# Loads reordered at the start of an attention-plus-experts kernel, and a last tile split 384 + 128

## The chip, the cores and the metric

The kernel runs on one core of a Trainium2 chip. The core has a matrix engine (TensorE, "PE" in the profile, with "PEld" for its weight loads), a vector engine (VectorE, "DVE"), an engine for activation functions (ScalarE, "ACT"), a general one (GpSimd, "POOL") and one that only issues transfers (SyncE, "SP"). Transfers between the device memory (DRAM) and the on-chip memory run on 16 DMA engines. TensorE writes its results into PSUM, from where VectorE or ScalarE copy them out. Each engine goes through its own instructions in order and waits where data or a buffer is missing. The metric is the time of one execution on the device in microseconds, as the median of several runs.

## What is computed

Attention over 4 batches, 8 heads, 768 positions and 64 channels per head, followed by a mixture of four experts over all 3072 tokens:

```python
scores = (q @ k.T) / sqrt(64)             # per batch and head
# heads 0, 2, 6: causal; heads 1, 3, 4, 5, 7: the first 4 keys and the last 64 alone
a = softmax(where(mask, scores, -1e9))
x = (a @ v), heads side by side           # 3072 x 512
p = domain_probs / domain_probs.sum(-1)   # 3072 x 4
for e in range(4):
    h = relu(x @ w1[e])                   # 512 -> 1024
    out += p[:, e] * (h @ w2[e])          # 1024 -> 512
```

All inputs are 32-bit floats; the weights, queries, keys and values are turned into 16-bit floats on their way into the chip.

## The kernel before

The tokens are worked on in eight groups of 384 (half a batch each). A *unit* is one group with one expert: a first layer of 32 matmuls of 384 columns (line L895), 16-bit results of which ScalarE writes as `hs` after the ReLU, and a second layer of 24 matmuls of 512 columns (L919), whose result VectorE scales and adds into `acc`. Group 0's attention comes first, alone; each later group's attention is dealt out between the matmuls of the group before it.

GpSimd issues the loads that change the type. The order in which they stand in the program is their order in one queue. `landed` makes GpSimd wait until a tile is there, so that not too many loads stand in the queue at once:

```python
load_v(0, 0, [2, 1, 3, 4, 6])
load_w1(0, 0, F)                # expert 0, first layer: two loads of 512 KB
load_v(0, 0, [5, 7])            # values of heads 5 and 7, group 0
load_w2(0)                      # expert 0, second layer: 1024 KB
# [...] memory set to zero and to ones
load_w1(1, 0, F)
landed(w1_of(0))
load_triples(k, k16, 0, 1)      # group 1's keys, 384 KB
load_triples(q, qt16, 0, 1)     # group 1's queries, 384 KB
landed(w2_of(0))
load_w2(1)
landed(qt16[0:1, 0, 0, 0:1])
load_v(0, 1, RH)                # group 1's values, heads 0, 2, 6
load_w1(2, 0, F)
landed(w2_of(1))
load_v(0, 1, SH[:2])
load_w2(2)
# [...]
```

Group 0's attention ends with the values of heads 5 and 7. `warm_up` puts matmuls on a tile of zeros ahead of some of them, which keep TensorE occupied while it would wait for data; their results are not used:

```python
def values(h):
    # [...]
    if first:
        warm_up(ps, {3: 4, 4: 4, 5: 6, 7: 10}.get(h, 0), 256)
    # [...] matmuls of v_tile and es (L726), then Ln, Exp and a scaling: xT

yield from values(5)
x_transposes(6)                 # head 6's result turned round (L703)
yield from values(7)
```

Group 1's attention begins by turning its queries and keys round on TensorE (L516), two heads at a time. The results of the first two pairs go to the pool `pV`, which has two buffers; VectorE copies them out (queries L525; keys L532 and L548):

```python
def transposes(hp):
    for x, is_k in ((qt16, 0), (k16, 1)):
        ps = bank() if hp > 1 else pV.tile([P, 512], FP32, name="pV", bufs=2)
        # [...] six matmuls against the identity (L516)
        if not is_k:
            nc.vector.tensor_copy(out=qTs[...], in_=...)   # L525
            yield t_ns
            continue
        # [...] two copies per pair, to kR (L532) or kS (L548)
        yield 2 * t_ns
```

`bank()` is the pool `pA` with four buffers, which scores and first layers share. Where group 1's attention begins and ends among group 0's units is set in the main loop; a `UNIT` is the nominal time of one unit, and each step of the attention is let in when the matmuls so far have passed its share:

```python
begin = {0: 1.15, 1: 1.0}.get(g, 0.0) * UNIT
end = {0: 3.5}.get(g, 0.90 * n_units) * UNIT
```

Group 2's keys are turned round by the DMA engines (`kR<-kRr`), as are those of all later groups.

The last tile of the last unit is made in two parts, so that the first part is scaled and stored while TensorE makes the second:

```python
def last_tile(e, nt, hs, acc):
    for n, eng in enumerate((nc.sync, nc.scalar)):
        cols = slice(n * DM // 2, (n + 1) * DM // 2)
        # [...] eight matmuls of 256 columns (L863)
        # [...] VectorE: acc += p * ps (L870)
        eng.dma_start(out=out[nt * P : (nt + 1) * P, cols], in_=acc[:, cols])
```

Of the kernel before, what the change touches and what calls it, by code (L numbers as in the profile page):

```python
# [17 lines left out]
def kernel(  # L18
# [33 lines left out]
    nc = tc.nc  # L52
    P = 128
    B, H, S, D = q.shape
    E, DM, F = moe_w1.shape
# [101 lines left out]
    def own_v(h):  # L157
        return half(PLACE[h][1])
# [10 lines left out]
    def v_tiles(b, c, h):  # L169

        if RETR[h]:
            return vR[b % 2][:, 3 * c : 3 * c + 3, RH.index(h), :]
        if b:
            return windows(vSf, c)[:, :, SH.index(h), :]
        return vS[:, c, :, SH.index(h), :]
# [10 lines left out]
    def rows_of(x, b, h, c):  # L186
        return x[b, h, c * CH : (c + 1) * CH, :].rearrange("(j p) d -> p j d", p=P)

    def tiles_of(x, b, h, c):
        return x[b, h, c * CH : (c + 1) * CH, :].rearrange("(t r) d -> r t d", r=TK)  # L190

    def windows_of(x, b, h, c):

        assert b > 0
        first = ((b * H + h) * S + c * CH - WO) * D
        return bass.AP(x.tensor, x.offset + first, [[D, P], [WQ * D, WT], [1, D]])
# [13 lines left out]
    def load_triples(x, dst, b, c):  # L210

        gp.dma_start(
            out=dst.rearrange("p h j d -> p h (j d)"),
            in_=x[b, :, c * CH : (c + 1) * CH, :].rearrange(
                "h (p j) d -> p h (j d)", j=3
            ),
        )
# [47 lines left out]
    def load_v(b, c, heads):  # L265
        for h in heads:
            t = v_tiles(b, c, h)
            if RETR[h]:
                gp.dma_start(out=t[:, :, 0:D], in_=rows_of(v, b, h, c))  # L269
            elif b:  # L270
                gp.dma_start(  # L271
                    out=t[:, :, own_v(h)], in_=windows_of(v, b, h, c)
                )
            else:
                gp.dma_start(  # L275
                    out=t[R0:P, :, own_v(h)],
                    in_=tiles_of(v, b, h, c),
                )
# [18 lines left out]
    def load_w1(e, f0, f1):  # L297
        x = moe_w1[e].rearrange("(u c d) f -> u d c f", u=2, c=DMP)
        for u in range(2):
            gp.dma_start(  # L300
                out=w1sb[half(u), e * DMP : (e + 1) * DMP, f0:f1],
                in_=x[u, :, :, f0:f1],
            )

    def load_w2(e):
        gp.dma_start(
            out=w2sb[:, e * FTP : (e + 1) * FTP, :],
            in_=moe_w2[e].rearrange("(fo fi) d -> fi fo d", fi=P),
        )
# [41 lines left out]
    for h in range(H):  # L351
        if h == 2:
            nc.sync.dma_start(
                out=v_s32, in_=v[0, :, 0:NS, :].rearrange("h r d -> r h d")
# [13 lines left out]
        eng = nc.scalar if h < HP else nc.sync  # L368
        eng.dma_start(out=q32[:, :, h, :], in_=rows_of(q, 0, h, 0))
    nc.sync.dma_start(  # L370
        out=probs, in_=moe_domain_probs.rearrange("(t p) e -> p t e", p=P)
# [14 lines left out]
    def warm_up(ps, n, cols):  # L386
        for _ in range(n):
            nc.tensor.matmul(
                out=ps[:, 0:cols], lhsT=warm[:, 0:P], rhs=warm[:, 0:cols],
                start=True, stop=True,  # L390
            )
# [53 lines left out]

    mask_c(bC, 0.0, -60000.0)
    mask_s(bS[:, 0:2, :], 2, 0.0, -60000.0)
    load_v(0, 0, [2, 1, 3, 4, 6])
    load_w1(0, 0, F)
    load_v(0, 0, [5, 7])  # L450
    load_w2(0)
    zero(gp, kR[0][:, 1, :, :, :])
    zero(gp, kS[:, 1, :, :, :].rearrange("p t s x -> p s t x"))
# [2 lines left out]
    qt16 = att.tile([P, H, 3, D], FP16, name="q16", bufs=2)  # L456

    def landed(x):

        gp.tensor_copy(out=seen, in_=x)  # L460

    def w1_of(e):
        return w1sb[D : D + 1, e * DMP, 0:1]

    def w2_of(e):
        return w2sb[0:1, e * FTP, 0:1]

    load_w1(1, 0, F)
    landed(w1_of(0))
    load_triples(k, k16, 0, 1)  # L470
    load_triples(q, qt16, 0, 1)
    landed(w2_of(0))
    load_w2(1)
    landed(qt16[0:1, 0, 0, 0:1])
    load_v(0, 1, RH)
    load_w1(2, 0, F)
    landed(w2_of(1))
    load_v(0, 1, SH[:2])
    load_w2(2)
# [15 lines left out]
    def attention(b, c):  # L495
        g = b * NCH + c
# [212 lines left out]
        def values(h):  # L709
            if RETR[h]:  # L710
                yield from values_r(h)
                return
            ct, u = PLACE[h]
            if first and u == 1:
                ps = pO.tile([P, 512], FP32, name="pO", bufs=2)
            else:
                ps = pV.tile([P, 512], FP32, name="pV", bufs=2)
            if first:
                warm_up(ps, {3: 4, 4: 4, 5: 6, 7: 10}.get(h, 0), 256)
            work = []  # L720
            for es, parts in es_of[h]:
                for t, o, q0, nq in parts:
                    work.append((es, t, o, q0, nq))
            ns = 0
            for n, (es, t, o, q0, nq) in enumerate(work):
                nc.tensor.matmul(  # L726
                    out=ps[:, q0 : q0 + nq],
                    lhsT=v_tile(b, c, h, t),
                    rhs=es[:, o : o + nq],
                    start=(n == 0),  # L730
                    stop=(n == len(work) - 1),
                    skip_group_check=True,
                )
                ns += mm_ns(nq)
                if ns > 300 and n < len(work) - 1:
                    yield ns
                    ns = 0

            r, o = half(u), half(1 - u)
            pair = first and h in (3, 4)  # L740
            if not pair or u == 0:
                rc_of[0] = att.tile([P, CH], FP32, name="rc", bufs=4)
            rc = rc_of[0]
            nc.scalar.activation(  # L744
                out=rc[r, :], in_=ps[o, 0:CH], func=AF.Ln, bias=eps[o, :]
            )

            def scale(r=r, ps=ps):
                nc.vector.tensor_tensor(  # L749
                    out=xT[g][r, ct, :], in0=ps[r, 0:CH], in1=rc[r, :], op=ALU.mult  # L750
                )

            if not pair:
                nc.scalar.activation(out=rc[r, :], in_=rc[r, :], func=AF.Exp, scale=-1.0)  # L754
                later(scale)
            elif u == 0:
                scale_of[0] = scale
            else:
                nc.scalar.activation(out=rc, in_=rc, func=AF.Exp, scale=-1.0)
                later(scale_of[0])  # L760
                later(scale)

            yield ns + (600.0 if g == 1 else 0.0)
# [92 lines left out]

    def last_tile(e, nt, hs, acc):

        for n, eng in enumerate((nc.sync, nc.scalar)):
            cols = slice(n * DM // 2, (n + 1) * DM // 2)  # L860
            ps = pV.tile([P, 512], FP32, name="pV", bufs=2)
            for ft in range(FTP):
                nc.tensor.matmul(  # L863
                    out=ps[:, 0 : DM // 2],
                    lhsT=hs[:, ft, 2 * P : 3 * P],
                    rhs=w2sb[:, e * FTP + ft, cols],
                    start=(ft == 0),
                    stop=(ft == FTP - 1),
                )
            nc.vector.scalar_tensor_tensor(  # L870
                out=acc[:, cols], in0=ps[:, 0 : DM // 2],
                scalar=p_sb[:, nt, e : e + 1], in1=acc[:, cols],
                op0=ALU.mult, op1=ALU.add,
            )
            eng.dma_start(out=out[nt * P : (nt + 1) * P, cols], in_=acc[:, cols])


    acc = {}
# [88 lines left out]
    UNIT = FTP * DMP * mm_ns(CH) + 3 * FTP * mm_ns(DM)  # L967
    for g in range(G):
        nxt = g + 1
        n_units = len(units[g])  # L970
        att_steps = iter(())
        if nxt < G:
            att_steps = attention(nxt // NCH, nxt % NCH)
        loads(g + 2)

        begin = {0: 1.15, 1: 1.0}.get(g, 0.0) * UNIT
        end = {0: 3.5}.get(g, 0.90 * n_units) * UNIT

        att_ns = 3500.0 if nxt % NCH == 0 else 5600.0
        if nxt < NCH:  # L980
            att_ns += 1100.0 + HP * 3 * 400.0 + NSH * 600.0
        spent = 0.0
        done = 0.0
        to_transpose = g + 2 < G
        for ns, share in moe_steps(units[g]):

            spent += ns * (share if g == 0 else 1.0)
            tick(ns)
            if to_transpose and spent > {0: 0.9, 1: 0.75}.get(g, 0.5) * n_units * UNIT:
                dma_transposes(*divmod(g + 2, NCH))  # L990
                to_transpose = False
            while done < (spent - begin) / (end - begin) * att_ns:
                step = next(att_steps, None)
                if step is None:
                    break
                done += step
                tick(step)
        for ns in att_steps:
            tick(ns)
        tick(LAG)  # L1000
# [35 lines left out]
```

The softmax here doesn't subtract the row's maximum and nothing guards it: scores larger than these inputs give would overflow.

## Time and profile before

| what | value |
|---|---|
| time, median of 3 runs | 398.83 us (398.28 to 398.88) |
| span of the profiled execution | 397.1 us |
| first layers, L895, 1024 matmuls | 185.9 us busy, 0.1 us idle before them |
| second layers, L919, 760 matmuls | 179.0 us busy, 0.8 us idle before them |
| loads issued by GpSimd | 102656 packets, 20.98 MB |
| granted TensorE clock | full |

The profile is of one execution. "Busy" is the time in which an engine works on an instruction; the time before an instruction in which the engine stood still is put down to the instruction or transfer that released it. In a timeline each row has the start in us from the beginning of the span, the duration, the engine, the line of the program, the operation with the tiles that it writes and reads, and how many such instructions follow each other ("x8"). Matmuls overlap their neighbours, so the distance between starts tells more of their cost than the duration of one. The chain of waits is followed back from the last instruction: at each step to what released it.

### The profile page before, as it was taken

The numbers are of one execution on the slowest core, as the hardware profiler recorded it, in microseconds if no ns is written. First come the engines' busy times: TensorE is split into PE (matmuls) and PEld (weight loads), VectorE is DVE, ScalarE is ACT, GpSimd is POOL, SyncE is SP. The second block draws the span as 40 slices with busy tenths as digits, with TensorE's granted clock in tenths as the row PEclk, the third lists the DMA queues.
The fourth block names the chain that finished last, engine by engine and source line by source line (L and its number), as shares of the span: only waits on it lengthen the run. The fifth ranks groups of instructions, "written<-read, shape, count | busy, mean of one in ns | idle before, by whom it ended". The sixth has DMA issues, their size and how long they took to land.

```text
span 397.1 us, 7140 instructions
## 1 busy us (share of the span) xinstructions
PE 388.2 (98%) x2829; PEld 220.7 (56%) x2829; DVE 156.0 (39%) x344; ACT 219.0 (55%) x468; POOL 143.7 (36%) x184
## 2 busy tenths in 40 slices
PE   7899999999999999999999999999999999999996
PEld 4654556545555555555555555555555555555553
DVE  7734765324442234434332333433443223422222
ACT  4754569444766546655765446745564456853331
POOL 8833796808908706900049202940000000000000
PEclk9999999999999999999999999999999999999999
DMA  9999999999999999970779959990472000020002
GB/s 172 158 208 192 178 197 172 139 199 128 128 191 149 121 149 106 141 90 12 141 80 175 65 99 118 112 153 12 83 117 83 2 12 1 11 79 2 0 2 80
DMA packets 166133, 42.23 MB, mean 106 GB/s; under 512 B 156396, under 2 KB 161108, under 8 KB 166100
## 3 DMA queue, kind: packets, MB, share of 16 engines
q0 software_dynamic: 102656, 20.98, 62.0%
q1 hardware_dynamic: 61700, 20.27, 26.5%
q10 hardware_dynamic: 1744, 0.52, 0.6%
q8 instruction: 22, 0.36, 0.4%
q14 instruction: 11, 0.09, 0.1%
HBM read 43.57 MB, written 6.29 MB: 126 GB/s over the span
## 4 chain that ended last, share of the span: by engine, by line
PE 78%; DMA 15%; POOL 6%; issue 1%; DVE 0%; POOLq 0%
PE pA L895 35%; PE pO L919 35%; DMA w1sb<-in_moe_w_dram 4%; DMA w2sb<-in_moe_w_dram 4%; PE pA L614 4%; DMA q<-in_q_dram 3%; DMA kR<-kRr 2%; POOL vR L269 2%; PE pV L726 1%; PE pV L662 1%; DMA vS<-in_v_dram 1%; POOL w1sb L300 1%; POOL vS L275 1%; POOL vS L326 0%; POOL q L201 0%
## 5 line engine op out<-in xcount | busy, mean ns | idle before, releaser
L895 PE MATMUL pA<-xT,w1sb 128*128 128x384 f16 x1024 | 185.9, 326 | 0.1
L919 PE MATMUL pO<-w2sb,hs 128*128 128x512 f16 x760 | 179.0, 379 | 0.8 <-DMA w2sb<-in_moe_w_dram 0.8
L908 ACT ACTIVATE hs<-pA 128x384 f16<-128x384 f32 x256 | 121.8, 492 | 94.9 <-PE pA L895 89.6
L895 PEld LDWEIGHTS <-w1sb 128*128 128x128 f16 x1024 | 95.8, 98 | 59.6 <-issue 0.5
L919 PEld LDWEIGHTS <-hs 128*128 128x128 f16 x760 | 70.7, 98 | 73.9 <-DMA w2sb<-in_moe_w_dram 1.2
L632 ACT ACTIVATE es<-pA 128x384 f16<-128x384 f32 (+2 forms) x122 | 60.1, 512 | 53.7 <-PE pA L614 52.4
L935 DVE SCALAR_TENSOR_TENSOR acc<-pO,p_sb,acc 128x512 f32<-128x512 f32 x71 | 53.3, 751 | 71.8 <-PE pO L919 71.3
L227 POOL DMA_DIRECT2D kSr<-in_k_dram x30 | 30.1, 1006 | 31.5 <-DMA kS<-kSr 22.1
L223 POOL DMA_DIRECT2D kRr<-in_k_dram x18 | 14.1, 785 | 67.7 <-DMA kR<-kRr 67.7
L749 DVE TENSOR_TENSOR xT<-pV,rc 64x384 f16<-64x384 f32 x37 | 20.5, 554 | 32.0 <-ACT rc L754 24.3
L271 POOL DMA_DIRECT2D vS<-in_v_dram x30 | 30.4, 1024 | 0.8 <-DMA q<-in_q_dram 0.8
L931 DVE TENSOR_SCALAR acc<-pO,p_sb 128x512 f32<-128x512 f32 x24 | 18.0, 751 | 28.8 <-PE pO L919 28.6
L636 DVE TENSOR_TENSOR es<-es,mC 128x256 f16<-128x256 f16 (+1 forms) x42 | 10.9, 258 | 45.4 <-ACT es L632 44.3
L744 ACT ACTIVATE rc<-pV,eps 64x384 f32<-64x384 f32 x37 | 21.3, 575 | 12.1 <-PE pV L726 11.5
L614 PE MATMUL pA<-qT,kR 128*128 128x384 f16 (+2 forms) x120 | 24.4, 278 | 0.9 <-ACT qT L525 0.4
L754 ACT ACTIVATE rc<-rc 64x384 f32<-64x384 f32 x38 | 19.8, 521 | 1.2
L269 POOL DMA_DIRECT2D vR<-in_v_dram x24 | 19.2, 802 | 0.4 <-issue 0.3
L726 PEld LDWEIGHTS <-vS 128*128 128x128 f16 x255 | 13.4, 98 | 7.7 <-DMA vS<-in_v_dram 2.1
L636 DVE TENSOR_TENSOR es<-es,mW 128x384 f16<-128x384 f16 x30 | 10.7, 358 | 16.9 <-ACT es L632 16.8
L614 PEld LDWEIGHTS <-kR 128*128 128x128 f16 x120 | 11.4, 98 | 10.6 <-DMA kR<-kRr 0.6
L662 PEld LDWEIGHTS <-es 128*128 128x128 f16 x252 | 13.2, 97 | 6.9 <-ACT es L632 0.6
L614 PEld LDWEIGHTS <-kS 128*128 128x128 f16 x255 | 13.3, 98 | 6.6
(102 smaller groups left out, 188.4 us busy)
## 6 DMA issues: line engine op xcount, KB each, us to landing
out_dram<-acc SPq DMA_DIRECT2D x23, 256.0 KB
w1sb<-in_moe_w_dram POOLq DMA_DIRECT2D x8, 512.0 KB, 9.4
w2sb<-in_moe_w_dram POOLq DMA_DIRECT2D x4, 1024.0 KB, 13.2
kSr<-in_k_dram POOLq DMA_DIRECT2D x30, 112.0 KB, 3.8
vS<-in_v_dram POOLq DMA_DIRECT2D x30, 112.0 KB, 5.6
q<-in_q_dram POOLq DMA_DIRECT2D x18, 128.0 KB, 4.3
vR<-in_v_dram POOLq DMA_DIRECT2D x24, 48.0 KB, 4.4
kRr<-in_k_dram POOLq DMA_DIRECT2D x18, 48.0 KB, 3.7
```

Source lines behind the costliest of these rows:

```text
L227: gp.dma_start(out=kSr[:, :, SH.index(h), own(h)], in_=windows_of(k, b, h, c),)
L269: gp.dma_start(out=t[:, :, 0:D], in_=rows_of(v, b, h, c))
L271: gp.dma_start(out=t[:, :, own_v(h)], in_=windows_of(v, b, h, c))
L614: nc.tensor.matmul(out=ps[:, o : o + nq], lhsT=key_tile(b, c, h, t), rhs=qTs[b, c][:, hp, q0 : q0 + nq], start=(n == 0 or not first), stop ...
L632: nc.scalar.activation(out=es[:, 0:cols], in_=ps[:, 0:cols], func=AF.Exp, scale=SC)
L636: nc.vector.tensor_tensor(out=es[:, o0:o1], in0=es[:, o0:o1], in1=m[:, mo : mo + o1 - o0], op=ALU.mult,)
L744: nc.scalar.activation(out=rc[r, :], in_=ps[o, 0:CH], func=AF.Ln, bias=eps[o, :])
L749: nc.vector.tensor_tensor(out=xT[g][r, ct, :], in0=ps[r, 0:CH], in1=rc[r, :], op=ALU.mult)
L895: nc.tensor.matmul(out=pss[ft][:, 0:CH], lhsT=w1sb[:, e * DMP + ct, ft * P : (ft + 1) * P], rhs=xT[g][:, ct, :], start=(n == 0), stop=(n = ...
L908: nc.scalar.activation(out=hs[:, ft, :], in_=ps[:, 0:CH], func=AF.Relu)
L919: nc.tensor.matmul(out=ps_o, lhsT=hs[:, ft, j * P : (j + 1) * P], rhs=w2sb[:, e * FTP + ft, :], start=(ft == 0), stop=(ft == FTP - 1),)
L935: nc.vector.scalar_tensor_tensor(out=acc[nt], in0=ps_o, scalar=p_ap, in1=acc[nt], op0=ALU.mult, op1=ALU.add,)
```

## The change

Five small edits. Head 5's first values are loaded ahead of expert 0's first weights instead of behind them, and only four instead of ten zero matmuls stand ahead of head 7's values. Expert 1's second weights are loaded ahead of group 1's keys and queries; the waits of GpSimd are set anew to fit, and expert 2's first weights come ahead of group 1's values. Group 1's attention begins at 1.4 instead of 1.15 units, since its queries and keys now come later. The last tile is split into 384 and 128 columns instead of 256 and 256, so that less is left to be scaled and stored after the last matmul.

```diff
-    load_v(0, 0, [2, 1, 3, 4, 6])
+    load_v(0, 0, [2, 1, 3, 4, 6, 5])
     load_w1(0, 0, F)
-    load_v(0, 0, [5, 7])
+    load_v(0, 0, [7])
     load_w2(0)
[...]
     load_w1(1, 0, F)
     landed(w1_of(0))
+    load_w2(1)
+    landed(w2_of(0))
     load_triples(k, k16, 0, 1)
     load_triples(q, qt16, 0, 1)
-    landed(w2_of(0))
-    load_w2(1)
-    landed(qt16[0:1, 0, 0, 0:1])
+    landed(w1_of(1))
+    load_w1(2, 0, F)
     load_v(0, 1, RH)
-    load_w1(2, 0, F)
     landed(w2_of(1))
[...]
-                warm_up(ps, {3: 4, 4: 4, 5: 6, 7: 10}.get(h, 0), 256)
+                warm_up(ps, {3: 4, 4: 4, 5: 6, 7: 4}.get(h, 0), 256)
[...]
-        for n, eng in enumerate((nc.sync, nc.scalar)):
-            cols = slice(n * DM // 2, (n + 1) * DM // 2)
+        for c0, c1, eng in ((0, 3 * P, nc.sync), (3 * P, DM, nc.scalar)):
+            cols = slice(c0, c1)
[...]
-        begin = {0: 1.15, 1: 1.0}.get(g, 0.0) * UNIT
+        begin = {0: 1.4, 1: 1.0}.get(g, 0.0) * UNIT
```

## The prediction, as written before the changed kernel ran

> **What bounds the kernel now.** I read the page first, then TensorE's waits, then the chain of waits, then the timelines of TensorE, GpSimd and VectorE for the first 90 us. The page's first part:
>
> ```profile
> PE 388.2 (98%) x2829; PEld 220.7 (56%) x2829; DVE 156.0 (39%) x344; ACT 219.0 (55%) x468; POOL 143.7 (36%) x184
> ```
>
> TensorE is busy for 388.2 of 397.1 us: all idle time together is 8.9 us. Only that, and the warm-up matmuls on zeros (busy, but no work), can be won. Three of TensorE's waits, with total, count and longest:
>
> ```profile
> PE pO L726 <- DMA vS<-in_v_dram: 1.2, 1, 1.2
> PE pO L919 <- DMA w2sb<-in_moe_w_dram: 0.8, 1, 0.8
> ...
> PE pA L614 <- DMA kR<-kRr: 0.2, 1, 0.2
> ```
>
> Head 5's first values cost 1.2 us, w2(1) costs 0.8, the keys of group 2 cost 0.2. All three releasers are transfers. The chain of waits (start, duration, what) shows that this is one story:
>
> ```profile
> 10.92 9.20 DMA w1sb<-in_moe_w_dram
> ...
> 21.30 13.45 DMA q<-in_q_dram
> ...
> 77.97 7.65 DMA kR<-kRr
> ...
> 85.67 0.39 PE pA L614 x2
> ```
>
> Up to 85.67 us the chain runs almost wholly through transfers and GpSimd's issues; only then does it go over to TensorE. So in the first 86 us the queue of loads paces the kernel and TensorE follows with little room; from there TensorE is the bound. The start of the work on TensorE (start, duration, instruction, idle time before):
>
> ```profile
> 18.33 0.82 PE L388 MATMUL pO<-warm 128*128 128x256 f16 x6
> 20.32 0.42 PE L726 MATMUL pO<-es,vS 128*128 128x160 f16 x4 [1.18 <-DMA vS<-in_v_dram]
> 20.58 0.33 PE L703 MATMUL pV<-ident,x_pair 128*128 128x128 f16 x3
> 20.75 1.25 PE L388 MATMUL pO<-warm 128*128 128x256 f16 x10
> 21.84 0.41 PE L726 MATMUL pO<-es,vS 128*128 128x160 f16 x4
> 22.09 5.75 PE L895 MATMUL pA<-xT,w1sb 128*128 128x384 f16 x32
> 27.68 5.34 PE L919 MATMUL pO<-w2sb,hs 128*128 128x512 f16 x24
> ```
>
> Six zero matmuls, the 1.18 us wait, head 5, ten zero matmuls (20.75 to 21.84, so 0.109 us each), head 7, and the first MoE unit at 22.09. And where w2(1) is waited for:
>
> ```profile
> 36.20 0.36 PE L516 MATMUL pV<-ident,q 128*64 128x128 f16 x6
> 36.49 0.82 PE L895 MATMUL pA<-xT,w1sb 128*128 128x384 f16 x4
> 37.25 0.36 PE L516 MATMUL pV<-ident,k 128*64 128x128 f16 x6
> 37.54 1.47 PE L895 MATMUL pA<-xT,w1sb 128*128 128x384 f16 x8
> 39.82 1.04 PE L919 MATMUL pO<-w2sb,hs 128*128 128x512 f16 x4 [0.81 <-DMA w2sb<-in_moe_w_dram]
> ```
>
> Group 1's first transposes of queries and keys lie inside unit 1's first layer; its second layer then stops until w2(1) is there at 39.8.
>
> **What the Trainium skill says.** "DMA: Bandwidth & Descriptors", section "Queues, rings and completion order": each DMA engine consumes the descriptors of a ring in order. The trace agrees. Issue time plus time to landing, from the answers by tile, gives: v5 20.3, v7 20.6, w2(0) 25.6, w1(1) 30.5, k 32.6, q 34.8, w2(1) 39.8. That is the order of issue, back to back: w2(0) and w2(1) take 5.0 us each, w1(1) 5.0, k and q 2.1 each. "TensorE: Matmul & The Clock Gate", section "What's actually happening": the clock falls to half after an idle window of about 3.4 us. This trace has no such idle time once TensorE is warm; after the 1.18 us wait the first layer still runs at 0.163 us per matmul (1.30 us for 8 in the chain). Its behaviour after 2 us of idling is shown by no run here.
>
> **The change, part by part.**
>
> Head 5's values ahead of w1(0): in the queue they leave the place behind w1(0) (landing 20.12) for the place ahead of it, so head 5 is there some 4 us before use. Head 7's load stays behind w1(0), with the same bytes ahead of it: 20.6 again. TensorE now goes: six zero matmuls from 18.33, 6 x 0.109 = 0.65, to 18.98; head 5, 0.26, to 19.24. The transposes of head 6 need x_pair; VectorE's timeline has it done at 19.26 + 0.36 = 19.62. They take 0.17, to 19.8; four zero matmuls, 0.44, to 20.23; head 7 waits for 20.6 and takes 0.25. The first unit begins at about 20.85 instead of 22.09: 1.24 us ahead.
>
> Fewer zero matmuls: six fewer, 6 x 0.109 = 0.65 us; these are part of that 1.24, not on top of it.
>
> w2(1) ahead of k and q: by the durations above, w1(1) lands at 30.6, w2(1) at 35.6, k at 37.7, q at 39.8. The set of bytes up to the last of the four is the same as before, so its end stays at 39.8; only which load comes last changes. TensorE: unit 0 takes 22.09 to 32.86 = 10.77 (it holds some short stops), so from 20.85 to 31.62; w1(1) is there. Unit 1's first layer is 32 x 0.1625 = 5.2, to 36.8 (some tenths more with the stops seen before); w2(1) is there too. The order of the built instructions puts q's transposes after four matmuls of the second layer (4 x 0.216 = 0.86): TensorE comes to them at about 37.7 and finds q missing until 39.8. The wait of 0.81 for w2(1) becomes one of about 2.1 for q. All of the head's 1.24 us is eaten.
>
> What is done at 39.8? Before: all of the first layer and two sets of transposes (0.29 each, 36.20 to 36.49). After: the first layer and four second-layer matmuls. So after is ahead by 0.86 - 0.58 = 0.28 us. That is all that is left of the gain.
>
> The attention that begins later has a price just after. Before, the first k transposes (37.25) and the second ones (40.98) lay 3.7 us apart, and VectorE had long made its copies in between. Now all four sets follow within 2.6 us. VectorE's rows for this chain:
>
> ```profile
> 41.19 0.80 DVE L525 CAST qT<-pV 128x384 f16<-128x384 f32 x1 [1.85 <-PE pV L516]
> 41.84 0.79 DVE L532 CAST kR<-pV 64x384 f16<-64x384 f32 x1
> 42.66 0.81 DVE L548 CAST kS<-pV 64x384 f16<-64x384 f32 x1
> ```
>
> One copy holds VectorE for 0.65 to 0.82 us. In the new order VectorE runs: query copy, an accumulation of the output (L935, 0.7), both key copies. From q at 39.8: copy at 40.2 (transposes to copy was 36.20 to 36.60), accumulation after the eighth second-layer matmul at 41.2, key copies at 41.9 and 42.7, done at 43.5. TensorE meanwhile does transposes 0.29, 4 x 0.216, transposes 0.29, 4 x 0.216, transposes 0.29: at 42.4 it wants the second set of keys, whose pool pV has two buffers, one still being read. It waits until 43.5: 1.1 us. Behind it eight score tiles go through the four banks of pA and ScalarE's 0.48 us per tile (3.81 for 8), now with less other work between; I put 0.2 us there.
>
> Sum up to group 1's first unit: -0.28 + 1.1 + 0.2 = +1.0. At the keys of group 2 TensorE waited 0.2 us; being late it need not wait: -0.2. That wait also bounds gains: the chain has kR landing at 85.62.
>
> The last part of 128 columns: TensorE does the same columns and ends at the same time. VectorE took 0.75 for 512 columns and 0.48 for 256, so 1.06 ns per column: 0.61 for 384 and 0.35 for 128. The 384 part is ready 1.30 us after the last tile's start instead of 0.87; VectorE takes it at 393.1 to 393.7 and the last part to 394.05. Before it ended at 393.99. The last store is half as large, but the first one is larger and leaves later: 0 to +0.1.
>
> Total: 398.83 + 1.0 - 0.2 + 0.05 = 399.7. The wait on VectorE is the least certain term, since a q that lands a little earlier, or a copy that overlaps better, shortens it; I weight it by one half to three quarters and predict 399.4.
>
> **Rivals.** First, as meant: both waits go and nothing replaces them. It would take 1.24 at the head and 0.8 at w2(1), about 396.8. For it speaks that w2(1) is indeed there in time; against it, q's place in the queue and the 85.62 us landing of group 2's keys, which would give back most of it: 398.0 to 398.6. Second, transfers hide it all: the wait only changes its name and VectorE's chain costs nothing, leaving -0.28 or less: 398.6. The equal byte count speaks for it. Third, the wait of 2 us plus 1.1 soon after lets the clock fall: an estimate from the page on the clock gate is half speed for one window of 3.4 us, 1.7 us lost: 401. Against it, the idle pieces are each shorter than the window.
>
> **Range and chances.** Rival two sets the middle of the lower side, the full sum plus some extra stalls the upper: 398.2 to 400.6. Every outcome is far inside 2% (8 us): faster 0.01, same 0.98, slower 0.01.
>
> **What would show it.** Right: the first unit at 20.7 to 21.0; no wait for vS at head 5; a wait of 1.7 to 2.5 us for q at L516 ending near 39.8; a wait of TensorE on VectorE's key copy near 42.4; no wait for w2sb; kR's wait gone; the end of VectorE within 0.1 us of before, counted from the last matmul. Wrong: q landing well before 39, which would make the gain real; or no wait at the second key transposes, which makes it rival two; or matmuls at half speed after the wait, rival three.

## The result and the profile after

The changed kernel took 401.71 us (median of 4 executions, 400.42 to 402.21), the kernel before 398.86 on the same chip: a ratio of 1.0068 (95% interval 1.0041 to 1.0094). It is slower, by 2.85 us; the prediction had said 399.4, at most 400.6. One of the four executions, the traced one, lay inside the range at 400.42, with a mean granted clock of TensorE of 1.000. The other three showed 0.995 or 0.996 and took 401.62 to 402.21. That difference is one part of the story; the trace of the 400.42 us execution tells the other.

TensorE's waits in it (total, count, longest):

```profile
PE pV L516 <- DMA q<-in_q_dram: 1.9, 1, 1.9
...
PE pV L516 <- DVE kS L548: 0.8, 1, 0.8
PE pV L662 <- ACT es L632: 0.8, 1, 0.8
```

The waits for head 5's values and for w2(1) are gone. In their place stand one for the queries and one for VectorE's key copy. Head 6's wait for ScalarE is older: it had 0.5 us before. The timeline of TensorE:

```profile
20.72 0.41 PE L726 MATMUL pO<-es,vS 128*128 128x160 f16 x4
20.97 0.49 PE L895 MATMUL pA<-xT,w1sb 128*128 128x384 f16 x2
...
37.20 1.03 PE L919 MATMUL pO<-w2sb,hs 128*128 128x512 f16 x4
40.12 0.36 PE L516 MATMUL pV<-ident,q 128*64 128x128 f16 x6 [1.90 <-DMA q<-in_q_dram]
40.41 1.04 PE L919 MATMUL pO<-w2sb,hs 128*128 128x512 f16 x4
41.38 0.36 PE L516 MATMUL pV<-ident,k 128*64 128x128 f16 x6
41.67 1.04 PE L919 MATMUL pO<-w2sb,hs 128*128 128x512 f16 x4
42.64 0.36 PE L516 MATMUL pV<-ident,q 128*64 128x128 f16 x6
43.82 0.36 PE L516 MATMUL pV<-ident,k 128*64 128x128 f16 x6 [0.83 <-DVE kS L548]
```

The first unit begins 1.12 us earlier (20.97 against 22.09). The second layer of unit 1 begins at 37.20 without a wait, so w2(1) is there. After four of its matmuls TensorE stands still until 40.12. The chain of waits names the same steps:

```profile
26.96 13.12 DMA q<-in_q_dram
40.08 0.04 issue
40.12 0.36 PE pV L516 x6
40.48 0.98 PE pO L919 x4
41.49 0.32 DVE acc L935
41.81 0.35 issue
42.16 0.78 DVE kR L532
42.94 0.03 issue
42.97 0.81 DVE kS L548
```

q lands at 26.96 + 13.12 = 40.08; then an accumulation (L935) stands on VectorE ahead of the two key copies, and they end at 43.8.

What each stage contributes is read from the starts of the units in the two traces:

| start of | before | after | difference |
|---|---|---|---|
| group 0, unit 0, first layer | 22.09 | 20.97 | -1.12 |
| unit 1, first layer | 32.86 | 32.00 | -0.86 |
| unit 2, first layer | 47.94 | 48.99 | +1.05 |
| unit 3, first layer | 62.77 | 64.05 | +1.28 |
| group 1, unit 0 | 74.30 | 76.04 | +1.74 |
| group 1, unit 2 | 96.95 | 98.34 | +1.39 |
| last tile | 391.56 | 392.95 | +1.39 |

All is decided between 32 and 98 us; after that both run in step.

### The profile page after: what moved, and what is told of

It is laid out like the page before. It is cut to its first block, busy times and chain, and to the rows that moved or that the text cites. A ratio compares the mean times of both kernels' runs of the same rounds, so it can differ in the third digit from the quotient of the medians.

```text
span 398.4 us, 7124 instructions
## 1 busy us (share of the span) xinstructions
PE 388.5 (98%) x2823; PEld 221.3 (56%) x2823; DVE 155.4 (39%) x344; ACT 219.0 (55%) x468; POOL 143.7 (36%) x184
## 4 chain that ended last, share of the span: by engine, by line
PE 88%; DMA 6%; POOL 3%; DVE 1%; ACT 1%; issue 0%; DVEq 0%; POOLq 0%
PE pO L919 39%; PE pA L895 39%; PE pA L614 5%; DMA q<-in_q_dram 3%; DMA w2sb<-in_moe_w_dram 3%; PE pV L726 2%; PE pV L662 2%; POOL vS L275 1%; ACT es L632 1%; POOL vR L269 1%; POOL bS L412 0%; PE pV L863 0%; POOL w1sb L300 0%; POOL k L212 0%; PE pA L516 0%
## 5 line engine op out<-in xcount | busy, mean ns | idle before, releaser
L935 DVE SCALAR_TENSOR_TENSOR acc<-pO,p_sb,acc 128x512 f32<-128x512 f32 x71 | 53.3, 750 | 70.9 <-PE pO L919 70.6
```

The lines of the kernel that those rows point to most:

```text
L935: nc.vector.scalar_tensor_tensor(out=acc[nt], in0=ps_o, scalar=p_ap, in1=acc[nt], op0=ALU.mult, op1=ALU.add,)
```

## The experiments

Medians of all runs, with the executions that had a mean clock of 0.998 or more apart from those at 0.997 or less. The kernel before was run beside each set: 399.31, 399.13 and 399.18 us, with a lower clock in 5 of 121 executions. The ratio is worked out over all executions and differs a little from the quotient of the two medians.

| kernel | median us | ratio to before (95% interval) | executions at full clock, median us | at lower clock, median us |
|---|---|---|---|---|
| changed, again | 401.67 | 1.0067 (1.0043 to 1.0091) | 2, 400.64 | 5, 401.70 |
| 16 zero matmuls in q's wait | 401.07 | 1.0039 (1.0030 to 1.0048) | 20, 401.08 | 0 |
| second transposes in pA | 401.24 | 1.0037 (1.0022 to 1.0052) | 5, 400.01 | 9, 401.37 |
| both of these | 400.31 | 1.0026 (1.0017 to 1.0036) | 9, 400.31 | 0 |
| order of loads and begin alone | 401.56 | 1.0061 (1.0040 to 1.0081) | 7, 401.48 | 5, 402.53 |
| begin at 1.7 | 399.72 | 1.0012 (0.9998 to 1.0025) | 12, 399.72 | 0 |
| ten zero matmuls at head 7 | 401.20 | 1.0044 (1.0031 to 1.0056) | 3, 400.87 | 3, 401.76 |
| 5 zero matmuls in q's wait | 401.25 | 1.0049 (1.0032 to 1.0066) | 3, 400.93 | 3, 401.77 |
| head alone | 398.83 | 0.9996 (0.9983 to 1.0008) | 12, 398.77 | 1, 400.31 |
| last tile alone | 399.45 | 1.0012 (1.0002 to 1.0022) | 13, 399.45 | 0 |
| some attention ahead of w2(1) | 398.51 | 0.9989 (0.9981 to 0.9997) | 21, 398.51 | 0 |
| the same, scores of head 0 first | 398.76 | 0.9984 (0.9974 to 0.9993) | 20, 398.75 | 0 |

My theory after the first result: the load queue paces the start, TensorE pays at q what it gained at the head, and the idling there makes the clock fall. The rivals: the lower clock is chance or comes from the zero matmuls that were taken out; or the head's gain is real and only q's place was wrong.

**Zero matmuls in q's wait.** The wait stays, the idling goes.

```diff
                     ps = pV.tile([P, 512], FP32, name="pV", bufs=2)
+                if g == 1 and hp == 0 and not is_k:
+                    warm_up(ps, 16, 256)
                 for j in range(3):
```

> The changed kernel with 16 matmuls on zeros (256 columns each, results unused) put directly ahead of group 1's first query transposes, so that TensorE stands still for about 0.2 us there instead of 1.9 us; every load and every other instruction is as in the changed kernel. Three of the changed kernel's four executions had a mean granted clock of 0.995 to 0.996 and took 401.6 to 402.2 us; the fourth had 1.000 and took 400.4. Theory (the 1.9 us of idling makes the clock fall for some microseconds): every execution has clock 1.000 and takes 400.2 to 400.7. Rival one (the six zero matmuls taken out at the head are what lets the clock fall): the clock still falls in most executions, 401.5 to 402. Rival two (the lower clock is chance and has nothing to do with idling): the same as rival one.

Its TensorE timeline at that place:

```profile
38.04 1.91 PE L388 MATMUL pV<-warm 128*128 128x256 f16 x16
40.84 0.36 PE L518 MATMUL pV<-ident,q 128*64 128x128 f16 x6 [0.89 <-DMA q<-in_q_dram]
```

Not one of 20 executions had a lower clock, against 5 of 7 and 3 of 4 of the changed kernel. The matmuls do no work and q comes no earlier, here at 40.8. So the idling causes the fall, and both rivals on the clock are out. The time, 401.07, is above the 400.7 expected, which was built on a q at 40.1 as in the first trace; in the other traces with the new order q lands between 40.3 and 41.1.

**The changed kernel again.** No edit.

> The changed kernel once more, unaltered, for a comparison on one chip with the three beside it. It should show two kinds of executions: about a third to a half at clock 0.999 to 1.000 with 400.4 to 401.0 us, the rest at 0.994 to 0.996 with 401.5 to 402.2; median 401.2 to 401.8, 2 us or more over the kernel before.

This time the traced execution was one with a fall. Busy times by stretch; the columns are the stretch, its length, the busy time of PE, PEld, DVE, ACT and POOL (with the count of instructions), the granted clock, the DMA share and GB/s:

```profile
36.92:40.33 3.41, 1.35 (x7) 0.48 (x5) 0.00 (x0) 1.15 (x4) 1.37 (x2) 1.00 1.40 204
40.33:43.75 3.42, 3.33 (x18) 1.30 (x19) 1.74 (x3) 0.00 (x0) 1.58 (x2) 0.50 1.19 205
```

and the rows behind it:

```profile
40.41 0.53 PE L516 MATMUL pV<-ident,q 128*64 128x128 f16 x6 [2.15 <-DMA q<-in_q_dram]
40.88 1.89 PE L919 MATMUL pO<-w2sb,hs 128*128 128x512 f16 x4
```

From 40.33 to 43.75 TensorE has half its clock: four second-layer matmuls take 1.89 us where the first trace shows 1.04. The clock falls just as work comes back, and stays down for 3.41 us. From q's transposes to unit 2 it takes 9.90 us here (40.41 to 50.31), against 8.87 in the first trace (40.12 to 48.99). The fall costs 1.03 us there: less than the 1.7 us of lost clock, in part because the wait for VectorE is 0.4 instead of 0.8 us. Executions with a fall are 1.06 us slower in the median (401.70 against 400.64, five and two executions). That figure is not the fall alone: q also landed 0.3 us later here than in the first trace, and a later q is what makes the wait longer.

**The second pair of transposes in the larger pool.**

```diff
-                if first or hp > 1:
+                if first or hp > 0:
                     ps = bank()
```

> The changed kernel, but group 1's second pair of transposes goes to the four-buffer pool pA instead of the two-buffer pool pV. Theory (at 43 us TensorE waits for the key copy only because pV has two buffers): the 0.83 us wait on the key copy goes, q's wait stays at 1.9 us, and an execution at full clock takes 399.6 to 400.0; if the q wait alone lets the clock fall, most executions still show 0.995 and lie 1.2 to 1.8 us higher; if both waits together are needed, the clock stays at 1.000. Rival (VectorE itself is the bound there): the wait only moves to the score matmuls that need the copied keys, and the time stays at 400.4.

The wait on the key copy is gone, the one for q stays (2.4 us in this trace), 9 of 14 executions show a fall, and those at full clock take 400.01. So q's wait alone is enough for the fall, and the pool with two buffers made the second wait. The clock by stretch here:

```profile
38.19:41.61 3.42, 1.30 (x12) 0.55 (x14) 0.80 (x1) 0.00 (x0) 1.55 (x2) 1.00 1.20 211
41.61:45.02 3.41, 3.41 (x24) 1.42 (x24) 2.84 (x4) 0.00 (x0) 0.69 (x1) 0.50 1.60 183
```

**Both together.** The two diffs above in one kernel.

> The changed kernel with the 16 zero matmuls ahead of group 1's first query transposes and with the second pair of transposes in pool pA, the two experiments of the first set together. If the waits and the clock add up, the clock stays at 0.998 to 1.000 in all executions and the time is 0.8 to 1.0 us under the changed kernel with the zero matmuls alone (401.07), so 400.1 to 400.3. If the key copy's wait only moves elsewhere, it stays at 401.0.

400.31, all nine executions at full clock: 0.76 us under the zero matmuls alone, or 0.5 by the ratios (1.0026 and 1.0039). From q's transposes to unit 2 it took 8.15 us (40.80 to 48.95) against 8.86 (40.84 to 49.70). The wait on VectorE's copy was therefore worth 0.5 to 0.8 us, and the two causes add up. A piece of it moved on: the scores now wait 0.3 us for a key copy. The version is still 1.2 us over the kernel before beside it. In its trace q lands at 40.76, where w2(1) landed at 39.78 in the kernel before, and 0.3 us lie outside the span (see the end).

**Order of loads and begin alone.**

```diff
-    load_triples(k, k16, 0, 1)
-    load_triples(q, qt16, 0, 1)
-    landed(w2_of(0))
     load_w2(1)
-    landed(qt16[0:1, 0, 0, 0:1])
-    load_v(0, 1, RH)
+    landed(w2_of(0))
+    load_triples(k, k16, 0, 1)
+    load_triples(q, qt16, 0, 1)
+    landed(w1_of(1))
     load_w1(2, 0, F)
+    load_v(0, 1, RH)
[...]
-        begin = {0: 1.15, 1: 1.0}.get(g, 0.0) * UNIT
+        begin = {0: 1.4, 1: 1.0}.get(g, 0.0) * UNIT
```

> The kernel before with the new order of loads and the later begin of the attention alone; the head with its ten zero matmuls, head 5's late values and the last tile are as before. Theory (the load queue ends with q at 40.1 whatever the head does, so the head's gain is lost there): the first unit begins near 22.1, q is waited for about 1.1 us instead of 1.9, again until about 40.1, the key copy is waited for 0.8 us, and the time at full clock is the changed kernel's, 400.3 to 400.7. With the shorter wait the clock should stay at 1.000. Rival (the head's change carries through to the end): about 1.1 us slower than the changed kernel at full clock, 401.5.

The first unit began at 21.95, as expected; q came only at 41.18 in this trace, so the wait was 2.24 instead of 1.1 us, and the time at full clock is above the 400.3 to 400.7 expected. In the time there is no sign of the 1.1 us by which the head of the changed kernel is ahead: the medians are 401.56 and 401.67. At full clock this one is slower (401.48 against 400.64, the latter from two executions only), so a part of the head may survive; the numbers don't settle how much. The lower clock came in 5 of 12 executions, against my expectation. This trace itself has none, although it has the longer wait:

```profile
36.52:39.93 3.41, 2.42 (x14) 1.11 (x12) 0.00 (x0) 1.91 (x6) 1.38 (x2) 1.00 1.42 203
39.93:43.35 3.42, 2.17 (x19) 1.01 (x20) 1.60 (x3) 0.00 (x0) 0.90 (x1) 1.00 1.19 204
```

The wait, 38.94 to 41.18, is split by a boundary of the stretches of 3.41 us at 39.93: 1.0 us of idling in one, 1.2 in the next.

**A later begin.**

```diff
-        begin = {0: 1.4, 1: 1.0}.get(g, 0.0) * UNIT
+        begin = {0: 1.7, 1: 1.0}.get(g, 0.0) * UNIT
```

> The changed kernel with group 1's attention beginning at 1.7 instead of 1.4 units, which puts the first query transposes after 16 instead of 4 of the second layer's matmuls. Theory (loads pace TensorE up to about 45 us): q's wait nearly goes, but TensorE then comes to unit 2's first layer before w1(2) is there (about 45.0) and waits 1 to 1.8 us for it; less attention is done by then, so the gain is small: 398.3 to 399.3 at full clock, and the clock may fall as the wait is about as long. Rival (only q's place in the order was wrong): no new wait, 397.5 to 398.3.

```profile
45.33 0.81 PE L895 MATMUL pA<-xT,w1sb 128*128 128x384 f16 x4 [1.11 <-DMA w1sb<-in_moe_w_dram]
```

q's wait went and the next load in the queue was waited for, as the theory says: TensorE meets the queue at another load. No execution had a fall; the longest idling in one stretch is 1.26 us in this trace. At 399.72 it is slower than my 398.3 to 399.3: group 1 began at 75.29 against 74.30 before, because the attention, squeezed into less time, ran into ScalarE (0.6 us) and smaller stops.

**The head alone**, on the kernel before.

```diff
-    load_v(0, 0, [2, 1, 3, 4, 6])
+    load_v(0, 0, [2, 1, 3, 4, 6, 5])
     load_w1(0, 0, F)
-    load_v(0, 0, [5, 7])
+    load_v(0, 0, [7])
[...]
-                warm_up(ps, {3: 4, 4: 4, 5: 6, 7: 10}.get(h, 0), 256)
+                warm_up(ps, {3: 4, 4: 4, 5: 6, 7: 4}.get(h, 0), 256)
```

> The kernel before with the head's two edits alone: head 5's values ahead of w1(0) and four zero matmuls ahead of head 7; loads, begin of the attention and last tile as before. Theory (the load queue ends w2(1) at 39.8 us whatever the head does): the first unit begins near 21.0, the wait for w2(1) grows from 0.8 to about 1.9 us and ends again near 39.8, and the time at full clock is the same as before within 0.3 us (398.9 to 399.3, where the kernel before had 399.31 in the first set); the clock falls in a part of the executions, which then take 1 to 1.5 us more. Rival (the head carries through): 1.1 us less, 398.2.

```profile
39.89 1.04 PE L919 MATMUL pO<-w2sb,hs 128*128 128x512 f16 x4 [2.24 <-DMA w2sb<-in_moe_w_dram]
```

The first unit began at 20.73, 1.36 us ahead of the kernel before; w2(1)'s wait grew from 0.81 to 2.24, that is by 1.43, and ended at 39.89 instead of 39.82. The time is the same (0.9996, and the interval from 0.9983 leaves no room for the 1.1 us of the rival). This shows most cleanly that the head's gain ends in the queue. The clock fell in one of 13 executions. In this trace the idling is again divided, with 0.48 us before and 1.76 after a boundary at 38.13:

```profile
38.13:41.54 3.41, 1.65 (x17) 0.79 (x18) 0.28 (x1) 0.24 (x2) 2.04 (x5) 1.00 1.50 175
```

Whether that holds for the other twelve is not known, as they were not traced.

**Ten zero matmuls kept.**

```diff
-                warm_up(ps, {3: 4, 4: 4, 5: 6, 7: 4}.get(h, 0), 256)
+                warm_up(ps, {3: 4, 4: 4, 5: 6, 7: 10}.get(h, 0), 256)
```

> The changed kernel with ten instead of four zero matmuls ahead of head 7's values, as before the change. Theory (the six zero matmuls only shift idling from the head to the wait for q, whose end is set by the queue): the first unit begins 0.6 us later, near 21.6, q is waited for about 1.4 us instead of 2.0, and nothing later moves: 400.4 to 401.0 us at full clock. Since no window of 3.4 us then holds 2 us of standing still, the clock falls in few or no executions, so the median is 0.6 to 1.2 us below the changed kernel's 401.67. Rival (taking the six out is a gain that reaches the end): 0.6 us slower than the changed kernel, 402.3.

At full clock 400.87 against 400.64: the six matmuls, 0.65 us at the head, make 0.2 at the end. As far as three and two executions can show, that part of the theory holds. The wait was not shorter, though: unit 0 ran 0.4 us faster in this trace (10.65 us, 11.03 in the changed kernel's first) and q came at 40.75, so TensorE waited 2.21 us and the clock fell, as it did in three of six executions. My "few or none" was wrong.

**Five zero matmuls in q's wait.**

```diff
-                    warm_up(ps, 16, 256)
+                    warm_up(ps, 5, 256)
```

> The changed kernel with five zero matmuls (0.55 us) ahead of group 1's first query transposes, where the first experiment had 16. It leaves about 1.5 us of standing still there. If the clock needs about 2 us of standing still in one window to fall, as the traced falls show (2.07 and 2.12 us, none at 1.90 or less), it stays at 0.998 to 1.000 in nearly all executions and the time is that of the 16 zero matmuls, 400.5 to 401.1. If any wait over 1 us is enough, most executions still show 0.994 to 0.996.

Three of six had a fall. It doesn't decide what it was made for: in the trace unit 0 was again the fast one and q late, so 2.45 us of idling were left instead of 1.5. It adds a fourth traced fall, again above 2 us.

**The last tile alone.** The last hunk of the diff.

> The kernel before with the last tile split 384 and 128 alone. From the traces: from the first matmul of the last tile to the end of the span it took 5.49 us with the old split and 5.38 with it in another run, 5.37 to 5.65 with the new one in six runs. Both theories of the start expect nothing here: the same as before within 0.2 us. A gain of more than 0.3 us would mean that part of the changed kernel's loss at the start is hidden by the tail.

1.0012 (1.0002 to 1.0022), 0.3 us slower by the medians. The trace shows no such loss in the tail, but it is of the fastest of the thirteen executions (398.95 us): from the first matmul of the last tile to the end of the span it took 5.46 us, 5.49 in the kernel before. VectorE's two parts end 1.50 + 0.88 = 2.38 us after that matmul, 2.43 in the kernel before:

```profile
391.71 1.91 PE L863 MATMUL pV<-w2sb,hs 128*128 128x384 f16 x16
391.91 0.75 DVE L935 SCALAR_TENSOR_TENSOR acc<-pO,p_sb,acc 128x512 f32<-128x512 f32 x1 [0.98 <-PE pO L919]
393.21 0.88 DVE L870 SCALAR_TENSOR_TENSOR acc<-pV,p_sb,acc 128x384 f32<-128x384 f32 x2 [0.55 <-PE pV L863]
```

Where the 0.3 us comes from is open; either way no gain of the split is seen.

**A version that gains.** If the queue cannot be hurried, TensorE needs other work while w2(1) is on its way. The head and the tail of the change stay, the order of loads is the old one with the begin at 1.15, the second pair of transposes goes to the larger pool, and a fifth of group 1's attention is let in early:

```diff
-            while done < (spent - begin) / (end - begin) * att_ns:
+            due = (spent - begin) / (end - begin)
+            if g == 0 and spent > begin:
+                due = max(due, min(0.215, (spent - begin) / (0.45 * UNIT)))
+            while done < due * att_ns:
[...]
-                if first or hp > 1:
+                if first or hp > 0:
```

> An attempt at a version better than both: the head's two edits and the new last tile on the kernel before, its order of loads kept, but about a fifth of group 1's attention (two pairs of transposes, the second in pool pA, and the scores of head 0) is let in ahead of the wait for w2(1) instead of behind it, so that TensorE has work while w2(1) is on its way. Theory (what is done when the transfer lands decides): the wait for w2(1) falls to 0 to 0.5 us, the second layer begins at 39.8 to 40.3 with 1.1 to 1.3 us more attention done than before, the clock stays, and the time is 0.5 to 1.1 us under the kernel before, unless the keys of group 2 (85.6) take part of it back. Rival (VectorE's copies of the transposed keys stop the scores at once): no gain, the wait moves to the scores.

```profile
38.65 0.76 PE L614 MATMUL pA<-qT,kR 128*128 128x256 f16 x5 [0.62 <-DVE qT L525]
40.10 0.81 PE L895 MATMUL pA<-xT,w1sb 128*128 128x384 f16 x4 [0.69 <-DVE kS L548]
40.75 3.62 PE L919 MATMUL pO<-w2sb,hs 128*128 128x512 f16 x16
```

No wait for w2(1) is left, all 21 executions kept their clock, and the ratio to before is 0.9989 (0.9981 to 0.9997): 0.4 us under the kernel before by the ratio, 0.6 by the medians. It is the first version that beats both kernels, if narrowly. It stands still for VectorE's copies instead, 1.5 us in three pieces, so the rival had half the truth.

**Scores of head 0 between the transposes.**

```diff
-                yield from transposes(1)
[...]
-                if not by_dma and n in (1, 3):
-                    yield from transposes({1: 3, 3: 2}[n])
+                if not by_dma and n in (0, 1, 3):
+                    yield from transposes({0: 1, 1: 3, 3: 2}[n])
```

> The better version of the second set, with the scores of head 0 between the first and the second pair of transposes instead of behind both. There TensorE stood still 0.2, 0.6 and 0.7 us for VectorE's copies of the second pair. Theory (what is waited for is VectorE's chain of six copies, 4.5 us): with the scores needing only the first pair's copies these waits go, the second layer begins when w2(1) lands (39.8 to 40.5), and the time is 0.2 to 0.6 us under the 398.51 of that version, about 398.1. Rival (w2(1)'s landing is what counts now): the waits only become one for w2(1) and the time stays at 398.5.

0.9984 (0.9974 to 0.9993), in time no different from the version before it (398.76 and 398.51). TensorE's waits on VectorE fell from 2.1 to 1.3 us over the whole trace, the first one for the zero tile aside. The traced execution is one of the slower ones (399.32 us), and its trace shows where that one lost the gain; of TensorE's waits the longest is now

```profile
PE pA L614 <- DMA kR<-kRr: 1.3, 1, 1.3
```

The keys of group 2, 0.2 us before, take back what was gained up to 84 us: group 1 began 0.65 us earlier than in the kernel before (73.65), its third unit 0.45 later (97.40). In the trace of the version before it, an execution of 398.05 us, group 1 began at 73.83 and TensorE did not wait for these keys at all; whether they cost anything in most executions is not shown.

## Why the prediction was wrong

**Where TensorE's time goes: right.** The first unit at 20.97 (predicted 20.85), no wait at head 5, w2(1) there in time, q's wait of 1.90 us (2.1) until 40.12 (39.8), the wait on the key copy of 0.83 (1.1). The order within a ring, for which the prediction cites the Trainium skill ("DMA: Bandwidth & Descriptors", section "Queues, rings and completion order"), is stated there in a paragraph on the queues of SyncE and ScalarE; for GpSimd's queue the traces show it: in all 14 its loads land in the order of issue.

**Sizes.** q's landing was 0.3 us too early in the sum, since I took the same end for the same bytes; in the nine traces with the new order it lies between 40.1 and 41.1. VectorE's wait was put 0.3 too high in the sum (1.1 for 0.83); the weighting, from 399.7 to 399.4, took that off again, and rightly: the experiment with both edits gives 0.5 to 0.8. The sum's +1.0 was meant for the start of group 1. At unit 2 the trace has +1.05, but that is luck: the 0.3 too little for q and the 0.3 too much for VectorE cancel there. At the start of unit 2 the changed kernel had also done less attention (one set of k transposes, 0.29, and three score matmuls, 0.17), and that work was still to come; the difference grew to +1.74 by group 1. Of this 0.35 was given back at group 2's keys and after (predicted 0.2). The last tile: 0.0 to -0.1 in the trace (0 to +0.1). In all +1.3 in the span at full clock, where the sum gave +0.85.

**Outside the span: not foreseen.** The time of an execution was longer than its span by 1.78 us (median) in the kernel before and in every kernel with the old order of loads, by 2.05 to 2.08 with the new order and the begin at 1.4, and by 1.92 with the begin at 1.7. That is another 0.3 us, from 1.78 to 2.06; no trace shows what it is.

**The step that failed: the clock.** The prediction rejected its third rival with "the idle pieces are each shorter than the window". The fall happened in 8 of 11 executions of the changed kernel. It cost 1.0 us in the trace above; in the four traces with a fall the way from q's transposes to unit 2 took 0.5 to 1.2 us longer than without one (9.90, 9.60 and 9.38 us against 8.87; with the larger pool 9.37 against 8.15). The Trainium skill's page "TensorE: Matmul & The Clock Gate" speaks of an idle window of about 3.4 us in its section "What's actually happening"; I read that as 3.4 us without a matmul. The traces confirm the length, since each of these four falls lasted 3.413 us and came a whole number of such stretches after the first rise of the clock, but not the reading: a stretch need not be empty. Three of the stretches that decide, in the changed kernel's first trace (no fall after it), with ten zero matmuls and with five (a fall after both); the second figure is the length, the third TensorE's busy time:

```profile
36.80:40.21 3.41, 1.51 (x12) 0.59 (x12) 0.00 (x0) 1.23 (x4) 1.39 (x2) 1.00 1.43 202
37.80:41.21 3.41, 1.20 (x11) 0.44 (x10) 0.06 (x1) 0.71 (x3) 0.89 (x2) 1.00 1.33 209
38.07:41.48 3.41, 0.96 (x12) 0.41 (x10) 0.34 (x1) 0.00 (x0) 1.17 (x2) 1.00 1.23 208
```

Between the first rise and the last matmul, idling in the worst stretch was 2.07, 2.12, 2.21 and 2.45 us in the four traces with a fall, and 1.90 (the changed kernel's first trace), 1.76 (the head alone), 1.29 or less in those without. The ends of the traces, where TensorE has no more work, fit as well: a last stretch with 1.97 us of idling was not followed by a fall (some attention ahead of w2(1)), one with 2.15 was (the last tile alone). The limit lies between 1.97 and 2.07 of 3.41 us here, and for a wait above it, where the boundaries fall decides: 2.24 us divided by one had no effect, 2.15 us of which 2.07 lay in one stretch did. This can explain why the same kernel shows both kinds of execution; two of its eleven were traced, and in the one without a fall the whole wait, 1.90 us, was under the limit.

For the traced execution with a fall the terms add up: 1.3 us in the span as in the first trace, 0.3 for its later q, 1.0 for the fall and 0.3 outside the span are 2.9, and it took 401.70 us against 398.83. The clock is the largest term but not the whole miss: with the 16 zero matmuls, without any fall, the changed kernel was still 1.6 to 1.8 us over the kernel before, where 0.6 had been predicted. Those are the sizes above.

**Still open:** why the head alone, with 2.24 us of waiting, had one fall in 13 and the new order of loads one in every two or so; why the kernel before, with no more than 1.2 us of idling in a stretch of its trace, shows a lower clock in 5 of 121 executions, none of them traced; the 0.3 us outside the span; and the 0.3 us of the last tile alone.

## What to carry to other kernels

While a queue of loads paces the start, moving one load ahead of another only changed the name of the wait here, and time won earlier on TensorE was lost again at the next load; what helped was other work that was ready. Before a wait is moved, work out what it merges with: one of 2 us or a little more cost 0.5 to 1.2 us beyond its length here, because TensorE's clock fell after a stretch of 3.4 us that held more than about 2 us of idling. If such a wait can't be avoided, matmuls on zeros inside it are worth a try: 16 of them kept the clock here in all 29 executions that had them.

## What the runs showed of the hardware

The clock fell at multiples of 3.413 us after its first rise (34.133 us after it in two traces, 37.547 in two), to one half, for 3.413 us, although TensorE was at work again for all or nearly all of them. The stretch before a fall held 2.07 us of idling or more; with 1.97 us or less there was none. Sixteen matmuls on zeros of 256 columns, 1.9 us, kept the clock up in all of 29 executions. Loads of the same bytes did not end at a fixed time: the last of w1(1), w2(1), k and q landed between 39.7 and 40.6 us in five traces with the old order and between 40.1 and 41.1 in nine with the new one, and w2(1) landed 4.4 to 5.8 us after the load ahead of it.
